# One load per group for batch 0: issued by SyncE, with GpSimd laying out q

## The chip, the cores and the metric

The kernel runs on one NeuronCore of one Trainium2 chip. The metric is the time on the device in microseconds (us), here the median of three runs. One execution was also taken by the hardware profiler; its rows are what the argument rests on. The engines are called by the names of the profile: PE is TensorE (PEld its weight loads), DVE is VectorE, ACT is ScalarE, POOL is GpSimd, SP is SyncE. SPq and ACTq are the instruction streams of SP and ACT where they issue DMAs: an engine that issues a DMA does nothing else in the meantime, and its stream is worked off in order.

## The reference

Two stages in fp32. First attention for 8 batches of 8 heads, 576 tokens, head size 64; heads 0 to 3 see the last 32 tokens, heads 4 to 7 every fourth of the last 128. Then a mixing over the sequence with rank 32 and a two-layer MLP with a residual:

```python
scores = scale * np.matmul(q, k.transpose(0, 1, 3, 2))
scores = np.where(masks[None, :, :, :], scores, -1000000000.0)
...
attn = attn / (np.sum(attn, axis=-1, keepdims=True) + 1e-09)
x = np.matmul(attn, v)          # laid out as [batch, token, head * 64]
h = xt @ U @ V                  # xt is x with tokens last
u = x + h.transpose(0, 2, 1)
return u + np.maximum(u @ w_ch1, 0.0) @ w_ch2
```

U, V, w_ch1 and w_ch2 arrive as 64-bit floats and are read as pairs of 32-bit words, so 16 MB of weights have to be narrowed on the chip.

## The kernel before, in words

**Work.** The 8 x 576 tokens are 36 tiles of 128, and the MLP takes three tiles at a time: 12 chunks, each a loop over 16 blocks f of the hidden layer (`layer1`, L821, and `layer2`, L838), all of it on PE in split precision (three products for each one). Attention of later batches, the mixing and the transposes are put between these matmuls by a queue of due times. So PE has the MLP as its main work from the first L821 to the end.

**Batch 0 comes first.** Nothing of the MLP can start before the first three tiles of x exist, so `first_batch` does batch 0 alone. Its heads are dealt into 9 groups g of 4 units; a unit is two blocks of 64 queries, one in the upper and one in the lower 64 rows of the contraction. For a group, PE multiplies q by k (L394, tile s), DVE masks and takes the row's extreme (L413), ACT takes the exponential (L417, tile p), PE transposes p (L428, tile ptp), ACT copies it to SBUF (L640, tile pt), PE multiplies by v (L451, tile pv), DVE divides (L457 to L481, `place`). The groups are pipelined on PE as s(g), ptp(g-1), pv(g-2). The results of groups 0 to 4 have to be scattered to token order by 24 small DMAs (x<-xp, L485) on SP. After group 7 come the rank-32 products (L517), the mixing (`mix`, L553 and L555) and the transposes of the first three tiles (`transp`, L584, L589, L590), and then the first L821.

**q in batch 0.** The two halves of q must stand in a block-diagonal form, so that the zero blocks keep the two query blocks apart. `q_sb` holds this form for all nine groups: two memsets (L751) clear it once, and two DMAs per group (L305) write the halves. In it the four units lie side by side, so a unit's 128 columns are read with a step of four elements.

**Loads and queues.** `load_q` (one DMA for k, L302, two for q, L305) and `load_v` (L313) are called for all nine groups ahead of everything else, and all of them are issued by ACT. So are all weight pieces: `fetch64` (L179, L181), with 5 raw buffers of which each is 512 KB for a piece. Piece 0 is U, 1 and 2 are V and the rest of U, from 3 on alternating blocks of the two weight matrices. SP issues the masks, the identity, the scatters, and for later batches q, k and v.

**Order.** Within `first_batch`, PE, DVE, ACT and SP keep an order worked out when the program is built; POOL's is by priority. A DMA that is issued waits first for the completion of one some eight DMAs before it, since completions are counted in eight slots shared by both queues (DMAHW0 to DMAHW7 in the rows below). A weight piece goes through ACT twice (L188, L189), DVE twice (L193, L195), and is split into a high and a low part by ACT or DVE (L199, L201) and POOL (L202).

Of the kernel before, what the change touches and what calls it, by code (L numbers as in the profile page):

```python
# [25 lines left out]
P = 128  # L26
# [61 lines left out]
U_AT = (5, 6)  # L88
ORDERED = {mybir.EngineType.PE, mybir.EngineType.DVE, mybir.EngineType.Activation, mybir.EngineType.SP}
# [48 lines left out]
def attention_moe_kernel(ctx: ExitStack, tc: tile.TileContext, q0, k0, qk1, qk2, vv, masks, wide, ident, ut, vt, uv, w1, w2, out):  # L138
# [28 lines left out]
    def fetch64(i):  # L167
        src, n = pieces[i][0], pieces[i][1]
        if 2 * F_LAST <= i - NSMALL:
            raw = [xpool.tile([P, DM], I32, tag="x", name=f"raw{i}_{h}") for h in range(2)]  # L170
        else:
            raw = [prep.tile([P, 2 * DM], I32, tag="raw", name=f"raw{i}", bufs=RAWS)]
        step = 2 * n // len(raw)
        out_ = []
        for h, r in enumerate(raw):
            r = r[:, 0:step]
            if len(src.shape) == 3:
                k = src.shape[1] // len(raw)
                nc.scalar.dma_start(out=r.rearrange("p (a b) -> p a b", a=k), in_=src[:, h * k:(h + 1) * k])  # L179
            else:  # L180
                nc.scalar.dma_start(out=r, in_=src[:, h * step:(h + 1) * step])  # L181
            words = r.rearrange("p (e w) -> p e w", w=2)
            out_.append((words[:, :, 0], words[:, :, 1], slice(h * step // 2, (h + 1) * step // 2)))
        return out_
# [115 lines left out]
    def load_q(g):  # L300
        t = early.tile([P, UNITS, KB], F32, tag="k", name=f"k{g}", bufs=NGB)
        nc.scalar.dma_start(out=t, in_=k0[g])  # L302
        for i in range(2):
            rs = slice(i * QB, (i + 1) * QB)
            nc.scalar.dma_start(out=q_sb[rs, g, i], in_=q0[g, rs])  # L305
        loaded[g, 0] = t

    def load_v(g, i):
        if (g, 1, i) in loaded:
            return  # L310
        if g < NGB:
            t = early.tile([KB, 2, UNITS, VW], F32, tag="v0", name=f"v{g}", bufs=NGB)
            nc.scalar.dma_start(out=t, in_=vv[g])  # L313
            loaded[g, 1, 0] = t[:, 0]
            loaded[g, 1, 1] = t[:, 1]
        else:
            t = work.tile([KB, UNITS, VW], F32, tag="v", name=f"v{g}_{i}", bufs=3)
            ins = nc.sync.dma_start(out=t, in_=vv[g][:, i])
            if g < NGB + 2:
                tc.keep_in_program_order(ins)  # L320
            loaded[g, 1, i] = t
# [47 lines left out]
    def score(g, u):  # L369
# [12 lines left out]
        else:  # L382
# [9 lines left out]
            else:  # L392
                ql, kr = q_sb[:, g].rearrange("p i (q u) -> p u (i q)", u=UNITS)[:, u], loaded[g, 0][:, u]
# [240 lines left out]
    def first_batch():  # L634
# [6 lines left out]

        for g in range(NGB):
            for u in range(UNITS):
                score(g, u)
# [52 lines left out]
        for i in range(0, 2 * TB, 2):  # L697
            fetch(N0 + i, nc.scalar)
# [50 lines left out]
    q_sb = early.tile([P, NGB, 2, UNITS * QB], F32, name="q_sb")  # L749
    for i, eng in enumerate((nc.gpsimd, nc.vector)):  # L750
        eng.memset(q_sb[i * QB:(i + 1) * QB, :, 1 - i], 0.0)  # L751
# [4 lines left out]
    nc.sync.dma_start(out=mask_sb, in_=masks)  # L756
    nc.sync.dma_start(out=id_sb, in_=ident)
    order = tc.manual_schedule(engines=ORDERED)
    order.__enter__()
    for g in range(NGB):  # L760
        load_q(g)
        load_v(g, 0)
# [104 lines left out]
def lay_out(q, k, v, U, V, w1, w2):  # L867
# [6 lines left out]
    for half in range(2):  # L874
# [13 lines left out]
        for i in range(NJ // 2):  # L888
            g = TILES.index((half, 2 * i)) // 2
            for r in (slice(0, D), slice(D, P)):  # L890
                qk2[:, g, :, r, :P] = qp[SPLIT:, :, P * i:P * (i + 1)].transpose(0, 1, 3, 2)
                qk2[:, g, :, r, P:] = kp[SPLIT:, :, P * i:P * i + KW].transpose(0, 1, 3, 2)
    q0 = np.ascontiguousarray(np.stack([q1[0, :, :, i, :, i] for i in range(2)], axis=2)
                              .transpose(0, 2, 3, 4, 1)).reshape(NGB, P, QB * UNITS)
    k0 = np.ascontiguousarray(k1[0].reshape(NGB, UNITS, P, KB).transpose(0, 2, 1, 3))
# [22 lines left out]
    for p in range(NDP):  # L918
# [7 lines left out]
        "q0": q0,  # L926
        "k0": k0,
# [27 lines left out]
```

## Time and profile before

| | us |
|---|---|
| median of 3 runs | 1048.17 (1044.62 to 1048.58) |
| time of the profiled execution | 1047.01 |
| its span, first to last instruction | 1045.1 |
| first score of batch 0 on PE (L394) | 5.95 |
| ACT's first instruction that isn't a DMA | 25.05 |
| last group's scores (g = 8) on PE | 49.91 |
| first matmul of the MLP (L821) | 68.83 |

Times in the profile count from the span's first instruction. The profiled execution took 1.9 us more than its span and is 1.2 us below the median. The granted TensorE clock is 0.986 of full speed over the span. In rows of the timeline the first number is the start, the second the time to the end of the group of merged instructions; brackets give the idle time of the engine before it, and what ended that.

### The profile page before, as it was taken

How to read it: one execution, taken by the hardware profiler on the slowest of the kernel's cores; microseconds unless marked ns; L12 is line 12 of the kernel's file. 1: busy time of each engine (PE TensorE's matmuls, PEld its weight loads, DVE VectorE, ACT ScalarE, POOL GpSimd, SP SyncE). 2: the span in 40 equal slices, each digit the busy share in tenths (PEclk: the TensorE clock that was granted, in tenths of full speed). 3: DMA queues.
4: the chain of work that ended last, by engine and by line, in shares of the span. 5: the costliest groups of instructions: out<-in, count | busy, mean ns of one | idle time of the engine just before them, and what ended most of it. 6: DMA issues, size and time to landing. Idle time of an engine off the chain costs nothing.

```text
span 1045.1 us, 17970 instructions
## 1 busy us (share of the span) xinstructions
PE 990.9 (95%) x5904; PEld 867.7 (83%) x5904; DVE 593.3 (57%) x1972; ACT 387.6 (37%) x946; POOL 298.6 (29%) x501
## 2 busy tenths in 40 slices
PE   1968897899999999999999999999999999999998
PEld 1847785788898888888888888988888888998997
DVE  1359938777536774666637775666737774311211
ACT  0568735434423451434414442434414442111110
POOL 1146613325203350325404351325304340000000
PEclk9989998899999999999999999999999999999999
DMA  9338654434223332434323332433323330400000
GB/s 229 107 119 280 194 161 122 124 101 121 69 67 100 111 98 54 123 95 115 99 67 96 96 109 52 130 97 110 100 70 95 93 91 22 125 1 1 31 1 31
DMA packets 98204, 102.08 MB, mean 98 GB/s; under 512 B 13088, under 2 KB 85984, under 8 KB 98112
## 3 DMA queue, kind: packets, MB, share of 16 engines
q1 hardware_dynamic: 82272, 77.53, 26.6%
q10 hardware_dynamic: 15840, 23.40, 7.3%
q8 instruction: 48, 0.79, 0.3%
q14 instruction: 44, 0.36, 0.1%
HBM read 78.86 MB, written 17.30 MB: 92 GB/s over the span
## 4 chain that ended last, share of the span: by engine, by line
PE 83%; DVE 3%; DMA 2%; issue 1%; ACT 1%; SPq 0%; ACTq 0%; DVEq 0%
PE acc L838 37%; PE ph L821 36%; PE pv L451 4%; PE s L381 3%; PE t L531 2%; PE m L553 1%; DMA raw<-w 1%; PE s L394 1%; DMA zd<-z 1%; DMA v<-vv 0%; DVE v L195 0%; DVE x L555 0%; DVE z L563 0%; PE ptp L428 0%; ACT v L188 0%
## 5 line engine op out<-in xcount | busy, mean ns | idle before, releaser
L838 PE MATMUL acc<-w2h,hh 128*128 128x512 f32 x576 | 229.7, 400 | 8.8 <-ACT hh L826 8.8
L838 PE MATMUL acc<-w2l,hh 128*128 128x512 f32 x576 | 229.3, 399 | 0.0
L827 DVE SCALAR_TENSOR_TENSOR hl<-ph,hh 128x384 fp32r<-128x384 f32 x192 | 106.1, 553 | 199.6 <-ACT hh L826 198.8
L838 PE MATMUL acc<-w2h,hl 128*128 128x512 f32 x576 | 211.3, 399 | 1.1 <-DVE hl L827 1.1
L358 POOL TENSOR_TENSOR qks<-qkr,qks 128x160 fp32r<-128x160 f32 x192 | 102.8, 535 | 367.7 <-ACT qks L357 259.2
L826 ACT ACTIVATE hh<-ph 128x384 fp32r<-128x384 f32 x192 | 93.3, 486 | 268.9 <-PE ph L821 257.4
L821 PE MATMUL ph<-utl,w1h 128*128 128x384 f32 x768 | 175.6, 341 | 0.0
L821 PE MATMUL ph<-uth,w1h 128*128 128x384 f32 x768 | 172.7, 343 | 1.6 <-DVE w1h L201 0.7
L821 PE MATMUL ph<-uth,w1l 128*128 128x384 f32 x768 | 171.8, 340 | 0.5 <-POOL w1l L202 0.5
L417 ACT ACTIVATE p<-p,nmax 128x160 f32<-128x160 f32 (+1 forms) x288 | 109.6, 406 | 132.5 <-DVE nmax L413 131.4
L821 PEld LDWEIGHTS ph<-uth,w1h 128*128 128x128 f32 x768 | 139.4, 191 | 18.7 <-ACT uth L589 1.6
L440 DVE STREAM_TRANSPOSE pt<-p 32x128 f32<-32x128 f32 x432 | 130.1, 301 | 18.7 <-ACT p L417 13.3
L821 PEld LDWEIGHTS ph<-uth,w1l 128*128 128x128 f32 x768 | 137.2, 190 | 1.2 <-POOL w1l L202 0.8
L821 PEld LDWEIGHTS ph<-utl,w1h 128*128 128x128 f32 x768 | 136.0, 189 | 1.7 <-issue 0.2
L838 PEld LDWEIGHTS acc<-w2h,hh 128*128 128x128 f32 x576 | 108.6, 189 | 26.8 <-ACT hh L826 10.6
L838 PEld LDWEIGHTS acc<-w2h,hl 128*128 128x128 f32 x576 | 107.7, 189 | 25.9 <-DVE hl L827 3.3
L838 PEld LDWEIGHTS acc<-w2l,hh 128*128 128x128 f32 x576 | 108.9, 189 | 16.7
L357 ACT CAST qks<-qkr 128x288 fp32r<-128x288 f32 x192 | 81.2, 429 | 95.8 <-PE s L381 53.6
L410 DVE TENSOR_TENSOR p<-s,wide_sb 128x160 f32<-128x160 f32 x192 | 60.1, 320 | 67.9 <-PE s L381 66.1
L361 POOL TENSOR_TENSOR qks<-qkr,qks 64x128 fp32r<-64x128 f32 x192 | 90.6, 472 | 15.0
L500 POOL TENSOR_TENSOR xhl<-x,xhl 128x256 fp32r<-128x256 f32 (+1 forms) x65 | 47.3, 736 | 98.3 <-ACT xhl L498 94.4
L413 DVE CUSTOM_DVE_ANT_0 p<-s,p 128x160 f32<-128x160 f32 x192 | 60.0, 321 | 4.1
(70 smaller groups left out, 868.3 us busy)
## 6 DMA issues: line engine op xcount, KB each, us to landing
qkr<-qk SPq DMA_DIRECT2D x192, 144.0 KB, 2.2
raw<-w ACTq DMA_DIRECT2D x26, 512.0 KB, 5.6
v<-vv SPq DMA_DIRECT2D x126, 97.5 KB, 2.2
out<-x SPq DMA_DIRECT2D x36, 256.0 KB, 2.3
zd<-z SPq DMA_DIRECT2D x120, 64.0 KB, 1.9
xt<-zd SPq DMA_DIRECT2D x30, 256.0 KB, 2.8
qkr<-qk SPq DMA_DIRECT2D x15, 224.0 KB, 4.1
x<-xp SPq DMA_DIRECT2D x96, 32.0 KB, 1.9
```

Of the source, the lines that this page charges most:

```text
L357: nc.scalar.copy(out=t[:, 0:QK2], in_=raw)
L358: nc.gpsimd.tensor_tensor(out=t[:, QK2:], in0=raw[:, P:], in1=t[:, P:QK2].bitcast(F32), op=ALU.subtract)
L361: eng.tensor_tensor(out=t[lo, 0:P], in0=raw[lo, 0:P], in1=t[lo, 0:P].bitcast(F32), op=ALU.subtract)
L410: nc.vector.tensor_tensor(out=p_sb[:, u, :], in0=sp[:, 0:KW], in1=wide_sb[:, kind], op=ALU.add)
L413: nc.vector.tensor_tensor_reduce(out=p_sb[rs, u, 0:w], in0=a, in1=c, scale=-1.0 / 8.0, scalar=3.0e38, op0=ALU.add, op1=ALU.min, accum_out= ...
L417: nc.scalar.activation(out=p_sb[:, u, 0:w], in_=p_sb[:, u, 0:w], func=AF.Exp, bias=nmax[:, u:u + 1], scale=-1.0,)
L440: nc.vector.transpose(out=pt[WIN * k:WIN * (k + 1), :, rs], in_=p_sb[rs, :, o:o + WIN])
L500: eng.tensor_tensor(out=xl[rs], in0=x[rs], in1=xh[rs].bitcast(F32), op=ALU.subtract)
L821: nc.tensor.matmul(ph, lhsT=w[:, k, :], rhs=u[:, k, :], start=(n == 0), stop=(n == len(seq) - 1))
L826: nc.scalar.activation(out=hh, in_=ph, func=AF.Relu)
L827: nc.vector.scalar_tensor_tensor(out=hl, in0=ph, scalar=0.0, in1=hh.bitcast(F32), op0=ALU.max, op1=ALU.subtract)
L838: nc.tensor.matmul(acc[i], lhsT=h[:, ss], rhs=w, start=(f == 0 and n == 0), stop=(f == FC - 1 and n == 2))
```

## The change

Host side: q's two halves and k of a group are laid into one array, `qk0`, as [group, row, unit, 64 of q + 96 of k]. On the chip `load_q` issues one DMA for it on SP instead of three on ACT. The DMA for v is issued by SP too, and so is every weight piece of the whole kernel (`fetch64`) and the first three loads of batch 1. The masks and the identity stay on SP, and now follow group 0's q and k in its stream.

`q_sb` becomes four buffers in rotation, cleared once, each [unit, half, 64], so that a unit's 128 columns lie next to each other. `spread_q` on POOL copies the two halves of a group from the loaded tile into its places; it is called one group ahead of the scores.

```diff
+NQ = 4
...
-                nc.scalar.dma_start(out=r.rearrange("p (a b) -> p a b", a=k), in_=src[:, h * k:(h + 1) * k])
+                nc.sync.dma_start(out=r.rearrange("p (a b) -> p a b", a=k), in_=src[:, h * k:(h + 1) * k])
             else:
-                nc.scalar.dma_start(out=r, in_=src[:, h * step:(h + 1) * step])
+                nc.sync.dma_start(out=r, in_=src[:, h * step:(h + 1) * step])
...
     def load_q(g):
-        t = early.tile([P, UNITS, KB], F32, tag="k", name=f"k{g}", bufs=NGB)
-        nc.scalar.dma_start(out=t, in_=k0[g])
+        t = early.tile([P, UNITS, QB + KB], F32, tag="k", name=f"k{g}", bufs=NGB)
+        nc.sync.dma_start(out=t, in_=qk0[g])
+        loaded[g, 0] = t
+
+    def spread_q(g):
         for i in range(2):
             rs = slice(i * QB, (i + 1) * QB)
-            nc.scalar.dma_start(out=q_sb[rs, g, i], in_=q0[g, rs])
-        loaded[g, 0] = t
+            nc.gpsimd.tensor_copy(out=q_sb[rs, g % NQ, :, i], in_=loaded[g, 0][rs, :, 0:QB])
...
-            nc.scalar.dma_start(out=t, in_=vv[g])
+            nc.sync.dma_start(out=t, in_=vv[g])
...
-                ql, kr = q_sb[:, g].rearrange("p i (q u) -> p u (i q)", u=UNITS)[:, u], loaded[g, 0][:, u]
+                ql, kr = q_sb[:, g % NQ, u].rearrange("p i q -> p (i q)"), loaded[g, 0][:, u, QB:]
...
+        spread_q(0)
         for g in range(NGB):
+            if g + 1 < NGB:
+                spread_q(g + 1)
             for u in range(UNITS):
                 score(g, u)
...
-            fetch(N0 + i, nc.scalar)
+            fetch(N0 + i)
...
-    q_sb = early.tile([P, NGB, 2, UNITS * QB], F32, name="q_sb")
+    q_sb = early.tile([P, NQ, UNITS, 2, QB], F32, name="q_sb")
     for i, eng in enumerate((nc.gpsimd, nc.vector)):
-        eng.memset(q_sb[i * QB:(i + 1) * QB, :, 1 - i], 0.0)
+        eng.memset(q_sb[i * QB:(i + 1) * QB, :, :, 1 - i], 0.0)
...
-    nc.sync.dma_start(out=mask_sb, in_=masks)
-    nc.sync.dma_start(out=id_sb, in_=ident)
...
         load_q(g)
+        if g == 0:
+            nc.sync.dma_start(out=mask_sb, in_=masks)
+            nc.sync.dma_start(out=id_sb, in_=ident)
         load_v(g, 0)
```

The line numbers of the changed kernel are 1 to 7 higher (L302 becomes L303, L394 becomes L397, L821 becomes L828). Three places show what moves in the engines' streams. Numbers behind a name tell buffers apart; k0 is the tile of group 0, p0 its exponentials, raw7 is weight piece 7.

The start of ACT's stream. Before, these rows stand behind 40 rows that issue DMAs, the last of which is shown first:

```order
L179 DMA raw5_164<-w1 128x4x256
L417 ACT_TABLE_LOAD
L417 ACTIVATE p0_166<-p0_166,nmax0_167 128x96 x4
L417 ACTIVATE p1_181<-p1_181,nmax1_182 128x96 x4
L640 COPY pt0_73<-ptp0_188 96x512
```

With the change they are the first rows after the branch into the program:

```order
L957 UNCONDITIONAL_BRANCH
L420 ACT_TABLE_LOAD
L420 ACTIVATE p0_152<-p0_152,nmax0_153 128x96 x4
L420 ACTIVATE p1_169<-p1_169,nmax1_170 128x96 x4
L643 COPY pt0_73<-ptp0_176 96x512
```

All DMA rows of the start have left ACT; what ACT computes keeps its order.

Weight pieces 7 and 8 before the first L821. Before, ACT's stream has their issues behind the three casts of the transposed tiles (uth, L589) and the first weight's high part:

```order
L589 CAST uth0_564<-tp1_576 128x4x128
L589 CAST uth0_564<-tp2_586 128x4x128
L199 CAST w2h_0_80<-v_4_543 128x512
L179 DMA raw7_595<-w1 128x4x256
L338 DMA qkr36_597<-qk1 128x448
L338 DMA qkr38_599<-qk1 128x448
L338 DMA qkr40_601<-qk1 128x448
L218 CAST us_71<-u32_88 128x4x32
L218 CAST us_71<-u32_88 128x32
L188 ACTIVATE v_2_607<-raw2_448 128x448
L189 ACTIVATE raw2_448<-raw2_448 128x448
L188 ACTIVATE v_5_631<-raw5_164 128x512
```

With the change SP's stream has them behind the last scatters, with the waits that stand before each:

```order
L488 DMA x3_265<-xp4_440 32x256 [waits DMAHW7_49]
L488 DMA x4_309<-xp4_440 16x256 [waits DMAHW0_49]
L182 DMA raw2_448<-uv 128x896 [waits DMAHW1_49,Pool_49]
L182 DMA raw6_450<-w2 128x1024 [waits DMAHW2_49,Pool_49]
L180 DMA raw7_595<-w1 128x4x256 [waits DMAHW3_49,Pool_49]
L341 DMA qkr36_597<-qk1 128x448 [waits DMAHW4_49]
L341 DMA qkr38_599<-qk1 128x448 [waits DMAHW5_49]
L341 DMA qkr40_601<-qk1 128x448 [waits DMAHW6_49]
L182 DMA raw8_639<-w2 128x1024 [waits DMAHW7_49,Pool_49]
L180 DMA raw9_728<-w1 128x4x256 [waits DMAHW0_49,DVE_49,Activation_49]
L182 DMA raw10_737<-w2 128x1024 [waits DMAHW1_49,Pool_49]
```

The pieces no longer wait for ACT's turn but for SP's: what SP has to wait for, the rows behind it wait for too, the loads of batch 1 (qkr) among them.

ACT's stream at the same place with the change:

```order
L190 ACTIVATE raw6_450<-raw6_450 128x512
L592 CAST uth0_564<-tp0_566 128x4x128
L190 ACTIVATE raw7_595<-raw7_595 128x512
L592 CAST uth0_564<-tp1_576 128x4x128
L190 ACTIVATE raw8_639<-raw8_639 128x512
L592 CAST uth0_564<-tp2_586 128x4x128
L200 CAST w2h_0_80<-v_4_543 128x512
```

The low words of pieces 6, 7 and 8 are now scaled ahead of and between the three casts that the first L821 waits for; before, pieces 7 and 8 came after it.

More of the change, by code (lines that the diff above doesn't have):

```diff
@@ L137, in attention_moe_kernel @@
 @with_exitstack
-def attention_moe_kernel(ctx: ExitStack, tc: tile.TileContext, q0, k0, qk1, qk2, vv, masks, wide, ident, ut, vt, uv, w1, w2, out):
+def attention_moe_kernel(ctx: ExitStack, tc: tile.TileContext, qk0, qk1, qk2, vv, masks, wide, ident, ut, vt, uv, w1, w2, out):
     nc = tc.nc
@@ L892, in lay_out @@
                 qk2[:, g, :, r, P:] = kp[SPLIT:, :, P * i:P * i + KW].transpose(0, 1, 3, 2)
-    q0 = np.ascontiguousarray(np.stack([q1[0, :, :, i, :, i] for i in range(2)], axis=2)
-                              .transpose(0, 2, 3, 4, 1)).reshape(NGB, P, QB * UNITS)
-    k0 = np.ascontiguousarray(k1[0].reshape(NGB, UNITS, P, KB).transpose(0, 2, 1, 3))
+    q0 = np.stack([q1[0, :, :, i, :, i] for i in range(2)], axis=2).reshape(NGB, UNITS, P, QB)
+    qk0 = np.concatenate([q0, k1[0].reshape(NGB, UNITS, P, KB)], axis=-1)
+    qk0 = np.ascontiguousarray(qk0.transpose(0, 2, 1, 3))
     qk1 = np.concatenate([q1.reshape(B, NGB, UNITS, P, P), k1.reshape(B, NGB, UNITS, P, KB)], axis=-1)
@@ L925, in lay_out @@
     return {
-        "q0": q0,
-        "k0": k0,
+        "qk0": qk0,
         "qk1": qk1,
```

## The prediction

> **What bounds the kernel now.** I read the page's slices first. The third row is ACT, the last the busy share of the 16 DMA engines; a slice is 26 us.
>
> ```profile
> span 1045.1 us, 17970 instructions
> ...
> PE   1968897899999999999999999999999999999998
> ...
> ACT  0568735434423451434414442434414442111110
> ...
> DMA  9338654434223332434323332433323330400000
> ```
>
> PE is full from the ninth slice on; in the first it does a tenth, and ACT nothing, while the DMA engines are at 9. The same by stages (columns: stretch, its length, then busy us of PE, PEld, DVE, ACT, POOL, the granted clock, DMA share, GB/s):
>
> ```profile
> 15.00:20.00 5.00, 0.00 (x0) 0.00 (x0) 0.00 (x0) 0.00 (x0) 0.00 (x0) 1.00 1.07 262
> 20.00:26.00 6.00, 0.00 (x0) 0.00 (x0) 0.00 (x0) 0.94 (x1) 0.00 (x0) 1.00 1.04 251
> ...
> 50.00:69.00 19.00, 12.63 (x95) 8.30 (x96) 9.30 (x34) 8.44 (x19) 4.45 (x4) 0.84 0.15 53
> 69.00:130.00 61.00, 51.24 (x297) 43.92 (x298) 56.88 (x119) 47.66 (x100) 39.53 (x31) 0.94 0.78 251
> 130.00:200.00 70.00, 59.15 (x360) 48.25 (x359) 45.34 (x142) 32.89 (x89) 21.28 (x30) 0.90 0.48 139
> 200.00:1045.00 845.00, 840.29 (x4961) 743.48 (x4959) 468.90 (x1596) 282.09 (x695) 227.31 (x426) 1.00 0.29 81
> ```
>
> From 200 us PE is busy for 840 of 845 us: what starts earlier there ends earlier, by the same amount. From 69 to 130 us DVE is the fullest (56.9 of 61); it narrows the weights. From 15 to 26 us no engine computes. The timeline and the list of waits say why.
>
> ```profile
> 5.95 2.16 PE L394 MATMUL s<-k,q_sb 128*128 128x96 f32 x8 [5.95 <-DMA q_sb<-q]
> ...
> 24.58 0.44 ACTq L179 DMA_DIRECT2D raw<-w  x1
> 25.05 1.28 ACT L417 ACT_TABLE_LOAD   x1 [25.05 <-DMA q_sb<-q]
> 26.35 2.23 ACT L417 ACTIVATE p<-p,nmax 128x96 f32<-128x96 f32 x8
> 26.78 1.24 PE L428 MATMUL ptp<-id_sb,p 128*96 128x128 f32 x4 [16.23 <-ACT p L417]
> 27.81 2.02 PE L394 MATMUL s<-k,q_sb 128*128 128x96 f32 x8
> 31.68 2.19 PE L394 MATMUL s<-k,q_sb 128*128 128x96 f32 x8
> 34.30 1.17 ACT L417 ACTIVATE p<-p,nmax 128x96 f32<-128x96 f32 x4 [1.83 <-DVE nmax L413]
> 38.80 2.11 PE L394 MATMUL s<-k,q_sb 128*128 128x96 f32 x8
> 41.89 2.11 PE L394 MATMUL s<-k,q_sb 128*128 128x96 f32 x8
> ...
> 49.91 2.11 PE L394 MATMUL s<-k,q_sb 128*128 128x96 f32 x8
> ...
> 68.83 1.65 PE L821 MATMUL ph<-uth,w1h 128*128 128x384 f32 x4 [0.68 <-ACT uth L589]
> ```
>
> Scores of groups 0 and 1 are there by 10.5 us, but ACT has all loads and three weight pieces to issue before it may compute, and each issue waits for an earlier DMA's completion. Its first exponential is at 26.35, PE's first transpose waits 16.2 us for it, and everything behind follows from there to the MLP's first matmul at 68.83. The bound of the first 26 us is ACT's stream, not the data of group 0.
>
> **Term 1: batch 0 starts without ACT's issues.** I walk the new start from the rows.
>
> ```profile
> v<-vv ACTq DMA_DIRECT2D x9, 195.0 KB, 4.4
> k<-k ACTq DMA_DIRECT2D x9, 192.0 KB, 4.7
> q_sb<-q ACTq DMA_DIRECT2D x18, 64.0 KB, 4.4
> ...
> mask<-masks SPq DMA_DIRECT2D x1, 240.0 KB, 3.3
> ```
>
> (Size of each DMA, and median us from issue to landing.) Group 0's q and k, 320 KB, are issued first, at about 0.7 us. An early 240 KB took 3.3 us, the later 192 KB took 4.7 in full traffic: I take 3.6, so 4.3 us. POOL then copies two halves of 64 x 256. No row has such a copy; POOL's nearest are these.
>
> ```profile
> 0.74 2.01 POOL L751 MEMSET q_sb<- 64x2304 f32 x1 [0.29 <-POOLq L946]
> ...
> 43.89 0.87 POOL L195 TENSOR_TENSOR u<-u,raw 128x320 int32<-128x320 int32 x1 [39.47 <-ACT raw L189]
> ...
> L361 POOL TENSOR_TENSOR qks<-qkr,qks 64x128 fp32r<-64x128 f32 x192 | 90.6, 472 | 15.0
> ```
>
> The memset goes at 0.87 ns a column, 0.22 us for 256; two-input operations take 2.7 to 3.7 ns a column, 0.7 to 0.9 us for 256. A copy reads one input: I take 0.5, bounds 0.22 and 0.9. Two are 1.0 us (0.45 to 1.8), so the scores of group 0 start at 5.3 instead of 5.95, those of group 1 when the first 2.2 us are over, 7.5. Group 0's exponentials: 2.6 us from a group's scores to the exponential's start (31.68 to 34.30), 1.2 for themselves, so 9.1, before the scores of group 1 end at 9.7. Then a transpose (1.1), and the scores of group 2 start at 10.8 instead of 27.81: 17.0 us earlier.
>
> Is the data there? Up to group 2's q and k stand 1654 KB with masks and identity; at 250 GB/s (the window from 20 us) that is 6.8 us, plus 2 for issue and landing, 8.8, and 9.8 after the copies: in time by 1 us. Up to group 8's they are 5448 KB with U and part of V: 22 us, 24 with landing, against about 30 when they are needed. The cover grows from group to group, so the transfers don't bound it. With a dearer copy (0.9) group 2 would be late by nothing, group 1 by 1 us. POOL's 18 copies are 9 us on an engine that idles from 4.5 to 43.9 us; they bind only if two take longer than a group's period.
>
> From group 2 to group 8 it was 22.1 us. PE's clock state stays as it was for the first ten us of work (3.87 us a group, against 3.09 from 38.80 on). What changes is the weight load of the scores, as q's columns now lie side by side:
>
> ```profile
> L394 PEld LDWEIGHTS s<-qkr x120: 186/192/192, 84.1 to 823.5; 128*128 128x128 f32 x120
> ...
> L394 PEld LDWEIGHTS s<-k,q_sb x72: 307/329/332, 5.9 to 51.5; 128*128 128x128 f32 x72
> ...
> 84.12 1.51 PE L394 MATMUL s<-qkr 128*128 128x96 f32 x12
> ```
>
> (ns, smallest/median/largest.) Twelve score matmuls with q side by side took 1.5 us in batch 1, so eight take 1.0 instead of 2.1. That is at most 1.1 us for each of four groups, 4.4. But ACT has 1.2 of exponentials, 0.6 of copy and in two groups 1.0 of narrowing, 1.8 to 2.8 a group, and comes to be the bound of a period near 2. I take 1.8 us, bounds 0 and 4.4. Group 8's scores end 18.8 us earlier.
>
> **What could hold it back up to the first L821.** The scatters on SP:
>
> ```profile
> 35.57 16.90 SPq L485 DMA_DIRECT2D x<-xp  x24
> ...
> 57.70 0.42 DVE L555 TENSOR_TENSOR x<-x,m 128x256 f32<-128x256 f32 x1 [1.39 <-PE m L553]
> ```
>
> 24 took 16.9 us, 0.7 each. They would start near 19 us, 3.9 behind the scores of group 3 as before (31.68, 35.57). But they now stand in one queue behind the loads and three weight pieces, and with eight slots the eighth of them waits until the last piece has landed. Loads and pieces together are 7179 KB, 29 us at 250 GB/s; the new loads have larger packets, so I take 28. Another 16 issues of 0.7 end at 39, landed by 41. The addition that needs them moves from 57.70 to 39: here a new wait of about 2 us comes up. Pieces 6, 7 and 8 follow the scatters on SP, and their first use now stands in ACT's stream before the casts that L821 waits for.
>
> ```profile
> 68.26 0.39 ACTq L179 DMA_DIRECT2D raw<-w  x1
> ...
> 70.43 0.33 ACTq L181 DMA_DIRECT2D raw<-w  x1
> ...
> 31.81 0.66 ACT L189 ACTIVATE raw<-raw 128x512 int32<-128x512 uint32 x1
> ...
> raw<-w ACTq DMA_DIRECT2D x26, 512.0 KB, 5.6
> ```
>
> Two more such activations are 1.3 us on that path, and piece 8, issued at about 46 after three loads of batch 1, lands at 51 to 52, when the last cast is due at 49.4 + 2. I charge 4 us for all this (2 for the scatters, 1.3, and the rest for piece 8), bounds 0 and 9 (a whole landing of 5.6 more than the scatters' 2 and the 1.3). Term 1: 18.8 - 4 = 15 us; first L821 at 54.
>
> **Term 2: weights in chunk 0.** Pieces 7 and 8 were issued at 68.26 and 70.43; now at about 44 and 46, that is 24 us earlier while the MLP starts 15 earlier. The MLP's second block would find its weights waiting, and DVE, which is the fullest engine of this stage, gets its work sooner. ACT also loses the issue of pieces 9 to 28, 0.35 us each, 7 us of a stage in which it is busy for 47.7 of 61: idle time of an engine that isn't the bound. I take 3 us, bounds 0 and 9, the difference of the two shifts.
>
> **Sum:** 1047.0 of the profiled execution - 15 - 3 = **1029 us**. The median of before is 1.2 higher, within the spread of its runs.
>
> The Trainium skill, "DMA: Bandwidth & Descriptors", section "Issuing engines are not separate DMA queues", says that DMAs of all issuers run on the same 16 engines, and that issuing from several saves only issue time, usually small beside the transfer. By that, moving them would gain almost nothing, 1046. The row of ACT's table load at 25.05 bears against it here, because issuing also holds up the engine's own work.
>
> **Rivals.**
>
> 1. *SP's stream holds batch 1 back, slower.* In chunk 0 the weight pieces now stand in one stream with q, k and v of batch 1, and wait for free raw buffers there.
>
> ```profile
> SPq L338 <- DMA raw<-w: 35.1, 4, 25.5
> ...
> qkr<-qk SPq DMA_DIRECT2D x15, 224.0 KB, 4.1
> ```
>
> If a load comes behind two pieces (5.6 us to landing against its own 4.1, and a buffer's wait), PE, which works in order, stands at the scores. Each of nine groups would have to lose more than 18 / 9 = 2 us to turn the sign. At 3 us a group the time is 1047 - 18 + 27 = 1056. Against it: in the order shown the loads stand close to where they stood in time, and SP had idle time there (35.1 us in the row).
>
> 2. *The one queue eats half of it ahead of L821.* Scatters and piece 8 come late to their bound, 9 us, q's layout is worth nothing, and term 2 nothing: 1047 - 17 + 9 = 1039. Here belongs a first copy that is late: the Trainium skill, "GPSIMD Engine Reference", section 2.1 "Instruction dispatch", tells of about 6 us for the first call into freshly loaded code. POOL's row at 43.89 stands behind 39 us of idle time and can't show such a wait; if it fell on group 0, the time by it would be about 1035.
>
> 3. *More than forecast.* All 9 us of term 2, the wait of 2 us for the scatters doesn't come up, and 2.6 more from q's layout: 1029 - 6 - 2 - 2.6 = 1018.
>
> 4. *No effect:* the loads, not their issue, set the pace, and batch 0 ends when it did. It would take group 8's data 20 us longer than now; 1047. The windows at 250 GB/s speak against it.
>
> **Chances.** Forecast 0.60; rival 3 0.14; rival 2 0.17; rival 1 0.06; rival 4 0.03. The range 1018 to 1040 holds all but the last two and the edges. About 0.5% (5 us) is what a measurement of this kernel tells from no change: faster 0.91, same 0.03, slower 0.06.
>
> **What would show it.** ACT's table load in the first 2 us; the scores of group 2 near 11, of group 8 near 30; weight loads of s near 190 ns at full clock; first L821 near 54; the stage to the end of chunk 0 not longer than before. It is wrong if PE waits at L397 for DMAs in chunk 0, if L821 comes after 60, or if PE isn't full from about 180 us on.

## The result, and the profile after

The changed kernel takes 1029.23 us (median of 4 runs, 1027.74 to 1031.81), the kernel before 1046.86 (4 runs, 1044.62 to 1048.58): ratio 0.9835, with a 95% interval of 0.9806 to 0.9865. The forecast was 1029. The profiled execution took 1031.81 us with a span of 1029.3, so it is the slowest of the four; another one had a span of 1025.8.

In the page's slices (25.7 us each; PE, ACT, DMA) the first slice of PE now shows 7 where it showed 1:

```profile
span 1029.3 us, 17998 instructions
...
PE   7589986999999999999999999999999999999998
...
ACT  5477445344233441434323541434323442111110
...
DMA  9558445343223422333233422334223421400000
```

The timeline of the start, with the rows that stood in the prediction for the kernel before (start, us, engine, line; L397 was L394, L420 was L417, L828 was L821):

```profile
0.74 1.28 ACT L420 ACT_TABLE_LOAD   x1 [0.74 <-PEq L952]
3.98 0.84 POOL L309 COPY q_sb<-k 64x256 f32<-64x256 f32 x2 [0.64 <-DMA k<-qk]
4.88 2.02 PE L397 MATMUL s<-k,q_sb 128*128 128x96 f32 x8 [4.88 <-POOL q_sb L309]
7.24 1.17 ACT L420 ACTIVATE p<-p,nmax 128x96 f32<-128x96 f32 x4 [5.21 <-DVE nmax L416]
7.74 0.85 POOL L309 COPY q_sb<-k 64x256 f32<-64x256 f32 x2 [2.92 <-DMA k<-qk]
11.32 1.86 PE L397 MATMUL s<-k,q_sb 128*128 128x96 f32 x8
14.87 1.13 PE L397 MATMUL s<-k,q_sb 128*128 128x96 f32 x8
...
25.38 0.86 POOL L309 COPY q_sb<-k 64x256 f32<-64x256 f32 x2 [2.06 <-DMA k<-qk]
26.34 0.87 POOL L196 TENSOR_TENSOR u<-u,raw 128x320 int32<-128x320 int32 x1
27.26 1.91 PE L520 MATMUL t<-xp,u 128*32 128x256 f32 x8 [1.54 <-POOL u L196]
29.10 1.13 PE L397 MATMUL s<-k,q_sb 128*128 128x96 f32 x8
...
53.17 1.65 PE L828 MATMUL ph<-uth,w1h 128*128 128x384 f32 x4 [0.68 <-ACT uth L592]
```

ACT's table load has gone from 25.05 to 0.74, the first exponential from 26.35 to 7.24, the scores of group 2 from 27.81 to 11.32, those of group 8 from 49.91 to 29.10, the first matmul of the MLP from 68.83 to 53.17. The stages (columns as in the prediction):

```profile
15.00:20.00 5.00, 5.00 (x64) 4.50 (x65) 2.95 (x22) 3.35 (x11) 1.58 (x4) 1.00 1.04 284
...
50.00:69.00 19.00, 13.96 (x49) 11.59 (x50) 15.29 (x22) 13.08 (x28) 13.23 (x12) 0.68 0.48 162
69.00:130.00 61.00, 58.88 (x379) 51.29 (x377) 50.51 (x131) 40.47 (x90) 30.84 (x24) 0.97 0.67 212
130.00:200.00 70.00, 57.31 (x337) 46.88 (x337) 49.89 (x152) 33.80 (x88) 24.56 (x38) 0.85 0.44 126
200.00:1029.00 829.00, 824.84 (x4859) 730.22 (x4857) 458.05 (x1555) 275.66 (x679) 221.38 (x414) 1.00 0.29 80
```

PE is now at work all of 15 to 20 us, where no engine computed. At the other end nothing changed: PE is busy for 824.8 of the last 829 us. The whole difference lies ahead of that. The timelines of all the kernels that were run give these points (us; "scatters" are those of batch 0 on SP, first start and end of the row; chunk 0 reaches from the first matmul of the MLP to that of chunk 1; "clock" is the granted TensorE clock over chunk 0, of full speed):

| kernel | table load | s of group 8 | scatters | first MLP matmul | chunk 0 | clock | span |
|---|---|---|---|---|---|---|---|
| before | 25.05 | 49.91 | 35.57, 52.47 | 68.83 | 126.7 | 0.93 | 1045.1 |
| before, second profile | 25.53 | 51.30 | 36.05, 53.81 | 70.27 | 126.1 | 0.93 | 1045.7 |
| after | 0.74 | 29.10 | 21.09, 41.27 | 53.17 | 126.5 | 0.89 | 1029.3 |
| after, second profile | 0.74 | 28.55 | 20.65, 41.10 | 53.17 | 123.9 | 0.93 | 1025.6 |
| issuer alone | 0.74 | 32.03 | 26.08, 44.13 | 56.54 | 129.0 | 0.90 | 1034.9 |
| merged and contiguous, on ACT | 17.26 | 36.34 | 26.57, 43.72 | 59.37 | 127.2 | 0.89 | 1035.8 |
| three transfers, contiguous, on SP | 0.74 | 30.86 | 28.73, 46.68 | 58.97 | 124.2 | 0.91 | 1032.2 |
| later pieces on ACT | 0.74 | 26.38 | 18.89, 39.93 | 52.25 | 130.6 | 0.89 | 1032.1 |
| first pieces on ACT too | 0.74 | 33.85 | 18.43, 38.76 | 51.02 | 130.0 | 0.91 | 1029.0 |
| scatters half on ACT | 0.74 | 40.76 | 21.18, 40.53 | 58.33 | 128.1 | 0.89 | 1036.1 |
| scatters half on POOL | 0.75 | 30.94 | 21.15, 33.46 | 55.21 | 126.6 | 0.90 | 1030.4 |
| additions left out | 0.74 | 27.61 | 20.82, 40.28 | 52.30 | 113.7 | 0.95 | 1014.6 |
| additions partly on POOL | 0.74 | 27.81 | 20.64, 40.64 | 52.84 | 127.5 | 0.89 | 1029.7 |
| neither hold | 0.75 | 29.95 | 20.42, 33.86 | 47.38 | 127.0 | 0.90 | 1023.5 |

From chunk 1's first matmul to the end of the span it is 848 to 850 us in each. Two kernels therefore differ by two lengths: the time up to the first MLP matmul, and chunk 0. The first was measured to 1.5 us by two profiles of the same kernel (68.83 and 70.27; 53.17 twice), the second to 2.6 us (126.5 and 123.9). In these last two the granted clock differs as well, 0.89 and 0.93; PE is busy for 108.7 and 105.8 us of chunk 0.

### The profile page after: what moved, and what is told of

The parts are those of the page before. It is cut to its first block, busy times and chain, and to the rows that moved or that the text cites. A ratio compares the mean times of both kernels' runs of the same rounds, so it can differ in the third digit from the quotient of the medians.

```text
span 1029.3 us, 17998 instructions
## 1 busy us (share of the span) xinstructions
PE 988.1 (96%) x5904; PEld 864.9 (84%) x5904; DVE 593.6 (58%) x1972; ACT 387.4 (38%) x946; POOL 306.7 (30%) x519
## 4 chain that ended last, share of the span: by engine, by line
PE 85%; DVE 2%; DMA 1%; ACT 1%; issue 0%; POOL 0%; DVEq 0%; SPq 0%; ACTq 0%
PE acc L845 38%; PE ph L828 37%; PE pv L454 4%; PE s L384 3%; PE t L534 2%; PE m L556 1%; PE s L397 1%; DMA raw<-w 1%; DVE v L196 1%; DMA zd<-z 0%; DVE v L194 0%; DVE x L870 0%; ACT v L189 0%; DVE z L566 0%; DVE x L558 0%
## 5 line engine op out<-in xcount | busy, mean ns | idle before, releaser
L834 DVE SCALAR_TENSOR_TENSOR hl<-ph,hh 128x384 fp32r<-128x384 f32 x192 | 106.2, 553 | 189.9 <-ACT hh L833 189.2
L828 PE MATMUL ph<-utl,w1h 128*128 128x384 f32 x768 | 176.6, 343 | 0.0
L828 PE MATMUL ph<-uth,w1h 128*128 128x384 f32 x768 | 172.7, 343 | 3.2 <-DVE w1h L202 1.6
L828 PE MATMUL ph<-uth,w1l 128*128 128x384 f32 x768 | 173.6, 342 | 0.7 <-POOL w1l L203 0.7
L420 ACT ACTIVATE p<-p,nmax 128x160 f32<-128x160 f32 (+1 forms) x288 | 109.8, 406 | 133.8 <-DVE nmax L416 132.4
L828 PEld LDWEIGHTS ph<-uth,w1h 128*128 128x128 f32 x768 | 139.5, 191 | 20.4 <-DVE w1h L202 1.8
L828 PEld LDWEIGHTS ph<-uth,w1l 128*128 128x128 f32 x768 | 138.0, 191 | 1.8 <-POOL w1l L203 1.0
L828 PEld LDWEIGHTS ph<-utl,w1h 128*128 128x128 f32 x768 | 137.5, 191 | 1.7 <-issue 0.2
```

Of the source, the lines that this page charges most:

```text
L420: nc.scalar.activation(out=p_sb[:, u, 0:w], in_=p_sb[:, u, 0:w], func=AF.Exp, bias=nmax[:, u:u + 1], scale=-1.0,)
L828: nc.tensor.matmul(ph, lhsT=w[:, k, :], rhs=u[:, k, :], start=(n == 0), stop=(n == len(seq) - 1))
L834: nc.vector.scalar_tensor_tensor(out=hl, in0=ph, scalar=0.0, in1=hh.bitcast(F32), op0=ALU.max, op1=ALU.subtract)
```

## Experiments: the two halves of the change

*Theory:* the gain is ACT's stream being free of issues. *Rival:* it is the transfers, their number and layout, and the issuer does not matter. The first kernel takes the issuer alone from the change:

```diff
-        nc.scalar.dma_start(out=t, in_=k0[g])
+        nc.sync.dma_start(out=t, in_=k0[g])
...
-            nc.scalar.dma_start(out=q_sb[rs, g, i], in_=q0[g, rs])
+            nc.sync.dma_start(out=q_sb[rs, g, i], in_=q0[g, rs])
```

and so for v, the pieces and batch 1's first loads; the masks and the identity follow group 0's loads as in the change.

> The first half of the change alone: everything that ACT issued before is issued by SyncE, but q keeps its own two transfers per group and its place with a step of four elements; GpSimd copies nothing. Theory 1 (freeing ACT's stream is what gains, the layout gives the 4 us between group 2's and group 8's scores): ACT's table load within 2 us, group 2's scores at about 12 us, group 8's at 33 to 34 instead of 29.1, first L821 of the MLP at 56 to 57, time 1032 to 1035. Theory 2 (fewer and larger transfers are what gains): batch 0 waits for its loads, first MLP matmul at 63 or later, 1041 to 1044.

Measured: 1035.79 us against 1051.31 of before on that chip, ratio 0.9872 (0.9836 to 0.9907). Theory 2 is out: the first MLP matmul came at 56.54, not at 63 or later. Group 2's scores came at 11.83 and group 8's at 32.03, 2.9 us behind the change's where theory 1 said 4, and the time is 0.8 us above its range. The second takes the merged load and POOL's copies alone, and ACT issues as before:

```diff
-        nc.sync.dma_start(out=t, in_=qk0[g])
+        nc.scalar.dma_start(out=t, in_=qk0[g])
```

> The second half alone: one transfer for q and k of a group and GpSimd's copies as in the change, but every load and weight piece is issued by ACT as before. Theory 1: ACT still has 23 issues ahead of its first exponential instead of 40; it comes at about 21 us instead of 26.4, group 8's scores at about 40, first MLP matmul at 59 to 60, time 1037 to 1040. Theory 2: most of the gain is here, 1030 to 1034.

Measured: 1036.42, ratio 0.9876 (0.9817 to 0.9936). ACT has 23 issues ahead of its first computation in place of 41 (the trace of the kernel before has 41, not 40), and its table load comes at 17.26:

```profile
16.84 0.39 ACTq L180 DMA_DIRECT2D raw<-w  x1
17.26 1.28 ACT L420 ACT_TABLE_LOAD   x1 [17.26 <-DMA raw<-vt]
```

The table load and group 8's scores (36.34) came some 4 us earlier than theory 1 said, the first MLP matmul (59.37) where it said; the 1030 to 1034 of theory 2 were not reached. So each half alone gives some three quarters of the ratio's gain (1.3 and 1.2 of 1.65%), and they overlap: both shorten the time until ACT may compute, one by taking the issues away, one by having fewer of them.

What does the merging add once SP issues? The third kernel keeps the change, but loads k and each half of q by a transfer of its own, contiguous, and has no POOL copies:

```diff
-        nc.sync.dma_start(out=t, in_=qk0[g])
+        nc.sync.dma_start(out=t, in_=qk0[g][:, :, QB:])
+        for i in range(2):
+            rs = slice(i * QB, (i + 1) * QB)
+            nc.sync.dma_start(out=q_sb[rs, g, :, i], in_=qk0[g, rs, :, 0:QB])
```

> The changed kernel with three transfers for each group's q and k, in place of one and two copies on GpSimd: k, and each half of q straight into its place beside the zeros (q's columns contiguous for TensorE as in the changed kernel, 64 float32 a packet); nine buffers in place of four, all issued by SyncE. If the merging matters (41 issues in place of 23 on SyncE, which after 8 of them waits for completions): the scatters start 4 to 5 us later than 21.1, as in the kernel where only the issuer was changed (26.1), the first matmul of the MLP comes at 55.5 to 57 in place of 53.2, and the time is 1032 to 1036. If q's layout was what that kernel lacked: its scores take 1.1 us for eight, group 8's scores come at 28 to 30, and the time is 1028 to 1031.

Measured: 1034.97, ratio 0.9862 (0.9838 to 0.9886). SP has to issue 1.83 us for each group's q and k:

```profile
24.59 0.55 SPq L303 DMA_DIRECT2D k<-qk  x1
25.18 1.28 SPq L306 DMA_DIRECT2D q_sb<-qk  x2
...
28.73 17.95 SPq L489 DMA_DIRECT2D x<-xp  x24
...
DVE x L559 <- DMA x<-xp: 7.3, 1, 7.3
```

(The last row is from the list of waits, us in total, times, longest.) Its scores are as early as the change's to within 2 us (30.86), but the scatters stand behind the 41 issues, start at 28.73 in place of 21.09 (7.6 us later, where 4 to 5 were expected), and DVE waits 7.3 us for them. Contiguous q makes a group 1.0 us shorter where the loads keep up (groups 3 to 5 follow every 2.1 us, and every 3.1 in the kernel with the issuer alone); groups 6 and 7 then wait 0.9 and 1.8 us for their q, so that 1.2 us are left at group 8's scores (32.03 to 30.86). The merging is worth 5.8 us at the first MLP matmul (58.97 to 53.17), more than the 2.3 to 3.8 expected. The bytes are the same; the delay stands in SP's row of issues. The forecast knew the issues as ACT's problem; on SP, too, they are a stream that something waits behind.

## Experiments: what holds the first MLP matmul back

Between group 8's scores and the first MLP matmul lie 18.9 us before and 24.1 after. These rows of the changed kernel's timeline show what is new there: DVE waits twice for scatters, and ACT three times for pieces 6, 7 and 8, whose low words it scales ahead of the three casts of uth.

```profile
38.19 0.42 DVE L558 TENSOR_TENSOR x<-x,m 128x256 f32<-128x256 f32 x1 [1.73 <-DMA x<-xp]
41.31 0.42 DVE L558 TENSOR_TENSOR x<-x,m 128x256 f32<-128x256 f32 x1 [1.29 <-DMA x<-xp]
...
46.30 0.65 ACT L190 ACTIVATE raw<-raw 128x512 int32<-128x512 uint32 x1 [3.74 <-DMA raw<-w]
...
48.31 0.68 ACT L190 ACTIVATE raw<-raw 128x512 int32<-128x512 uint32 x1 [0.88 <-DMA raw<-w]
...
51.35 0.67 ACT L190 ACTIVATE raw<-raw 128x512 int32<-128x512 uint32 x1 [1.08 <-DMA raw<-w]
```

That is 3.0 us on DVE and 5.7 on ACT. Two kernels change who issues the pieces, and when. In the first ACT issues piece 2 and those from 6 on:

```diff
+        eng = nc.scalar if i == 2 or i >= NSMALL + 3 else nc.sync
...
-                nc.sync.dma_start(out=r, in_=src[:, h * step:(h + 1) * step])
+                eng.dma_start(out=r, in_=src[:, h * step:(h + 1) * step])
```

> The change, but the second part of U and V and all weight pieces from 6 on are issued by ACT, in its stream where they stood before. Tells what the one queue costs ahead of the MLP, and what early pieces 7 and 8 are worth in chunk 0. Theory 1 (the early pieces are worth nothing and ACT's wait for them costs 2 to 3 us): first MLP matmul at 50 to 51 instead of 53.2, chunk 0 as long as before (126.5 us to the first matmul of chunk 1), time 1026 to 1028. Theory 3 (chunk 0 ends as its weights come): chunk 0 is longer by what L821 is earlier, 1029 to 1031.

Measured: 1031.34, ratio 0.9837 (0.98 to 0.9873). In the second ACT also issues the first three weight pieces, at group 4:

```diff
+        eng = nc.scalar if i >= 2 else nc.sync
...
+            if g == 4:
+                send(NSMALL + 3)
```

> As the kernel before it in this set, and the first three weight pieces are issued by ACT too, at group 4 of batch 0, so that SyncE's stream has only q, k, v and U ahead of the scatters. Theory 1: the scatters start at about 18.5 us instead of 21 and end by 36 instead of 41, DVE's wait of 3 us for them is gone, first MLP matmul at 48 to 49, time 1024 to 1027. Theory 3: chunk 0 gives it back, 1028 to 1031.

Measured: 1031.32, ratio 0.9834 (0.98 to 0.9869). The first MLP matmul comes 0.9 and 2.2 us earlier than in the change, both later than theory 1 said, and chunk 0 is longer by 3.5 us and more, as theory 3 said, so that the time can't be told from the change's. In the first, the casts of uth stand free of pieces, but ACT waits 3.1 us for piece 6 (sent at 30.13) further ahead, before its activation at 35.48. In the second, three issues on ACT, with the waits between them, take it from 20.31 to 25.04, and group 5's exponentials wait behind them; group 8's scores move to 33.85:

```profile
20.31 0.44 ACTq L181 DMA_DIRECT2D raw<-w  x1
...
24.61 0.39 ACTq L181 DMA_DIRECT2D raw<-w  x1
25.04 1.17 ACT L421 ACTIVATE p<-p,nmax 128x96 f32<-128x96 f32 x4 [4.24 <-DMA k<-qk]
```

By then the first MLP matmul had come 12 us behind the last scatter in four kernels (after 11.9, issuer alone 12.4, these two 12.3), which made SP's row of scatters look like the bound. Two kernels tested that; every second scatter of batch 0 goes to another engine, ACT in the one and POOL (`nc.gpsimd`) in the other:

```diff
-        for t, to, n, r in sorted(moves):
-            nc.sync.dma_start(
+        for k, (t, to, n, r) in enumerate(sorted(moves)):
+            eng = nc.scalar if b == 0 and k % 2 else nc.sync
+            eng.dma_start(
```

> The changed kernel, with every second one of batch 0's 24 scatters of the dilated half issued by ScalarE in place of SyncE. If SyncE's row of scatters (21.1 to 41.3 us) sets the first matmul of the MLP, which came 12 us behind the last scatter in four kernels: the last scatter goes out at about 36 to 38, the first matmul at 49 to 50 in place of 53.2, 3 to 4 us earlier. If something else sets it (ScalarE's row of exponentials and casts): the scatters end earlier and the first matmul stays at 53 or comes later, since 12 issues of 0.4 to 0.7 us are now in ScalarE's stream, 5 to 8 us. Time: 1025 to 1029 by the first, 1029 to 1036 by the second.

> The changed kernel with every second one of batch 0's 24 scatters issued by GpSimd in place of SyncE (on ScalarE they held the exponentials, as the loads did before). If the row of scatters sets the first matmul of the MLP: the last one goes out at 31 to 36 in place of 41.3, and the first matmul comes at 45 to 50, 3 to 8 us earlier than 53.2; the time is 1022 to 1027, as long as chunk 0 doesn't give it back. If the narrowing and the casts in ScalarE's row set it, the first matmul stays at 52 to 54 and the time at 1028 to 1031. If GpSimd's issues take 1.5 us or more each or hold its copies of q: later than 54.

Measured: on ACT 1037.54, ratio 0.9893 (0.9848 to 0.9938); on POOL 1033.01, ratio 0.9843 (0.9819 to 0.9867); the change on the same chip as the first 1029.42, ratio 0.9821 (0.978 to 0.9861). On ACT the issues stand in front of the exponentials, and group 8's scores go to 40.76: the kernel before in small.

```profile
22.35 2.84 ACTq L489 DMA_DIRECT2D x<-xp  x2
25.24 1.17 ACT L420 ACTIVATE p<-p,nmax 128x96 f32<-128x96 f32 x4 [7.62 <-DMA k<-qk]
...
26.81 4.11 ACTq L489 DMA_DIRECT2D x<-xp  x3
```

On POOL the scatters end 7.8 us earlier (13 on SP take 12.3 us), no DVE addition waits for them, and yet the first MLP matmul comes 2 us later, at 55.21. **The theory of the scatters falls**, and 55.21 lies in none of the three forecasts (GpSimd's issues took 0.5 us each, so they are not the reason for coming later than 54). In this kernel the order that is worked out at build time has the low word of piece 6 ahead of a cast of ts in ACT's stream, and ACT waits there for the piece; what made the order differ is not shown. Group 8's last pv and all behind it follow 4 us later, at half the clock (granted 0.50 from 38 us on, against 0.99 to 42 us in the change):

```profile
33.56 0.53 SPq L182 DMA_DIRECT2D raw<-uv  x1
34.18 0.38 SPq L182 DMA_DIRECT2D raw<-w  x1
...
38.44 0.65 ACT L190 ACTIVATE raw<-raw 128x512 int32<-128x512 uint32 x1 [4.07 <-DMA raw<-w]
...
40.13 1.14 PE L454 MATMUL pv<-v,pt 96*64 96x65 f32 x16 [4.18 <-ACT pt L644]
```

The wait for piece 6 stood there in the first kernel with pieces on ACT too. The new theory: two waits hold, the scatters in DVE's stream and the pieces in ACT's, and taking one away leaves the other. The last kernel takes both: half of the scatters on POOL, and the pieces from 6 on issued by ACT, the early sending of piece 6 dropped, so that no low word of theirs stands ahead of a cast.

```diff
+        eng = nc.scalar if i >= NSMALL + 3 else nc.sync
...
-        for t, to, n, r in sorted(moves):
+        for k, (t, to, n, r) in enumerate(sorted(moves)):
+            eng = nc.gpsimd if b == 0 and k % 2 else nc.sync
...
-                send(NSMALL + 4)
```

> The changed kernel with both waits between group 8's scores and the first matmul of the MLP taken out. Every second scatter of batch 0 goes over GpSimd, as in the run before, which ended the scatters at 33.5 in place of 41.3 and yet gave 55.2; and the weight pieces from the fourth on are issued by ScalarE behind the three casts of uth (the early sending of the fourth is dropped), so that no narrowing of them stands ahead of a cast. In the profile of the changed kernel VectorE waits 3.0 us for scatters there and ScalarE 5.7 us for pieces. If these two waits are the hold-back: 53.2 - 3.0 - 5.7 = 44.5, with TensorE at half its clock there 45 to 48. If only one of them counts, or the work itself at half the clock sets it: 50 or later. The weights then come later to chunk 0, and VectorE and GpSimd, which bound it, are late by as much: chunk 0 gives part of it back (126 to 132), and the time is 1021 to 1029; if it gives back all, as in the two kernels with pieces on ScalarE, 1029 to 1032.

Measured: 1024.90 us (5 runs, 1023.71 to 1026.72), ratio 0.9788 (0.977 to 0.9806).

```profile
41.27 0.58 ACT L594 CAST uth<-tp 128x512 fp32r<-128x512 f32 x1 [1.65 <-PE tp L589]
...
46.74 0.58 ACT L594 CAST uth<-tp 128x512 fp32r<-128x512 f32 x1 [2.26 <-PE tp L589]
...
47.38 1.65 PE L829 MATMUL ph<-uth,w1h 128*128 128x384 f32 x4 [0.68 <-ACT uth L594]
```

The three casts (at 41.27, 43.90 and 46.74) stand one behind the other with nothing of the pieces between, and the first MLP matmul comes at 47.38: 17.4 us behind group 8's scores in place of 24.1, 5.8 earlier than in the change and within the 45 to 48 expected. PE did not run at half its clock all the way (granted 0.88 between these two points, against 0.77 in the change), but that is a small part of it: the three groups of transposes ahead of the casts take 0.66, 0.89 and 1.11 us here and 1.11, 1.11 and 1.12 in the change, and in the change's second profile, at 0.66, the stretch is only 0.6 us longer (24.6). What the runs don't show is each wait's own share: no kernel takes the pieces' wait away and leaves the scatters as they were. Chunk 0 is 127.0, next to 126.5 and 123.9 in the change, so most of the gain stays. It is the fastest complete kernel of the study, about 4.4 us under the change by the medians; the two were not run on one chip, and their ratios to before lie side by side (upper end 0.9806, lower ends 0.9806 and 0.978), so the size of that step is less sure than its place in the trace.

## Experiments: what bounds chunk 0

Term 2 expected chunk 0 to become shorter by 3 us because its weights come earlier, and in the profiled pair it did so by 0.2. *Theory:* VectorE's work bounds it, not the arrival. One kernel leaves the low-word additions of w1 and w2 out:

```diff
-            add_low(i - 2, nc.vector)
+            narrow_b([], pipe[i - 2][1], nc.vector)
+            added.add(i - 2)
```

> The changed kernel without VectorE's additions of the weights' low words (the line `eng.tensor_tensor(... op=ALU.add)` for the pieces of w1 and w2; their shift stays). It leaves out the low words of the weights. In the changed kernel these additions stand between the shift and the casts, on the engine that is busy for 29 of 31 us at the head of chunk 0. If VectorE's work bounds chunk 0 (126.5 us from the first matmul of the MLP to the first of chunk 1, of which TensorE computes about 103): chunk 0 becomes shorter by 8 us or more, to 118 or less, and the run takes 1021 or less. If the arrival of the pieces bounds it (term 2 of the prediction): chunk 0 stays within 3 us of 126.5, and the run at 1026 to 1030. The start, up to the first matmul of the MLP, stays at 53.

Measured: 1018.17, ratio 0.9708 (0.9669 to 0.9747); chunk 0 113.7 us. Two windows of 31 us behind the start of chunk 0, first of the second profile of the change, then of this kernel:

```profile
53.00:84.00 31.00, 27.23 (x128) 24.30 (x129) 29.17 (x55) 24.47 (x52) 23.16 (x19) 0.88 0.70 231
84.00:115.00 31.00, 28.32 (x189) 23.88 (x187) 29.48 (x69) 23.27 (x50) 19.75 (x13) 1.00 0.71 221
```

```profile
53.00:84.00 31.00, 30.52 (x170) 27.39 (x170) 25.43 (x50) 29.84 (x63) 25.22 (x22) 0.95 0.93 307
84.00:115.00 31.00, 31.00 (x223) 26.90 (x222) 18.26 (x66) 18.65 (x44) 12.79 (x11) 1.00 0.56 172
```

With the additions DVE is at 29 of 31 and PE at 27 to 28; without them DVE falls to 25 and 18, and PE is full. Chunk 0 gets shorter by 10 to 13 us, as the theory said. Pieces 6 to 8 are sent as early as in the change, 11 to 9 us ahead of the first MLP matmul; the later ones follow sooner, the last by 7 us, since a piece waits for one of the five raw buffers and these come free as it is narrowed. So the narrowing on DVE bounds chunk 0, and with it the sending of most pieces. To gain from this with nothing left out, the next kernel gives every third of these additions to POOL:

```diff
-            add_low(i - 2, nc.vector)
+            add_low(i - 2, nc.gpsimd if i % 3 == 0 and i < NSMALL + 18 else nc.vector)
```

> The changed kernel with the low-word addition of every third of the first 18 weight pieces on GpSimd in place of VectorE. Leaving all of these additions out made chunk 0 shorter by 10 to 13 us (113.7). Six of them, 0.96 us each, are 5.8 us less on VectorE in chunk 0, and 6 times about 1.7 us, 10 us more on GpSimd, which is busy for 43 of the 62 us after the first matmul. If VectorE alone bounds the stage: chunk 0 at 118 to 121 in place of 124 to 126, the time 1023 to 1025. If the longer way of a piece over GpSimd binds instead (its subtraction of 1.5 us stands there too): chunk 0 at 124 or longer, 1029 to 1034.

Measured: 1032.21, ratio 0.9831 (0.9803 to 0.9858), chunk 0 127.5. It gains nothing, as the second forecast had it, and DVE's rows say why: four of the six additions fell into chunk 0, and from 53 to 145 us DVE's 20 remaining ones take 1163 ns each, against 1084 and 964 for 24 in the first and the second profile of the change.

```profile
L196 DVE CUSTOM_DVE_ANT_0 v<-raw,v 128x1024 uint16<-128x1024 uint16 x20 | 23.2, 1163 | 0.4
```

Four additions fewer, and 23.2 us of DVE where the two profiles of the change have 25.9 and 23.0. What stretches them is in the section on the hardware.

Two more runs show how far profiles of one kernel differ: the change and the kernel before once more.

> The changed kernel itself once more, beside the others on one chip: 1029 by all theories, first matmul of the MLP at 53, chunk 0 at 126.5 us. If chunk 0 differs by more than 1 us between two profiles of this kernel, differences of that size between the kernels are no evidence.

> The kernel before itself, profiled once more. Two profiles of the changed kernel gave 126.5 and 123.9 us for chunk 0, with the same first matmul of the MLP (53.17 both). By all theories: first matmul of the MLP at 68 to 70, the chain of the start as before (first exponential at 26). Term 2 compares chunk 0 of the two kernels: if this profile gives 126 to 127 again, the earlier weight pieces are worth 0 to 2.7 us; if it differs by 2 us or more from 126.7, the two kernels can't be told apart in that stage by single profiles.

Measured: the change 1029.42 (1028.09 to 1032.56), ratio 0.9821 (0.978 to 0.9861), chunk 0 123.9 where the first profile had 126.5; before 1047.36, ratio to itself 0.9982 (0.9959 to 1.0006), chunk 0 126.1 where it had 126.7. A difference of chunk 0 of up to 2.6 us between single profiles is therefore no evidence by itself.

## Why the prediction was right, and where it was not

- **What bounds the start: right.** The issuer alone brings the table load to 0.74 and 1.3% of the time, and wherever issues were put back on ACT (merged loads, the first pieces, half of the scatters) the exponentials behind them were late again by what the issues took. The sentence of the Trainium skill that was weighed ("DMA: Bandwidth & Descriptors", "Issuing engines are not separate DMA queues"), by which the time would be 1046, does not agree with the 1029.2 measured: it counts the issue time against the transfers, and here the cost was what stands behind the issues in the issuer's own stream.
- **Term 1, 15 us: right in sum** (15.7 at the first MLP matmul, 17.1 by the second profiles), from parts that err against each other: group 8's scores came 20.8 us earlier (18.8 forecast), and the hold-back behind them took 5.2 (4). That the total meets the forecast to 0.2 us is luck in this sense.
  - Group 2's scores came at 11.32 (10.8 forecast), the copies took 0.42 each (0.5), the first as soon as its load was there, so the wait for a first call on POOL that the second rival names did not show.
  - Group 8's came at 29.10 (about 30): 17.8 us behind group 2's in place of 22.1, so 4.3 us were gained there and not 1.8, nearly the upper bound of 4.4. The period near 2 came (2.1 us from group 3 to group 7), but ACT was not its bound: from 15 to 20 us PE is busy for all 5.0 us and ACT for 3.35. The slow first ten us of PE's work came too: its eight score matmuls take 2.02 us at 4.88, 1.86 at 11.32 and 1.13 from 14.87 on. But they now fall on groups 0 to 2, while before, behind the wait of 16.2 us, groups 2 and 3 were slow again (3.9 and 4.0 us in place of 3.1), and the prediction left that stretch in its 22.1. "The transfers don't bound it" failed too: POOL waits 2.9 us for group 1's load and 2.1 for group 8's, and as it works in order, the addition for U waits behind those copies, PE's t matmuls wait 1.5 us for U, and group 8's scores stand behind them. A copy whose data is late holds all that POOL has behind it; the prediction costed the copies but not what queues behind them.
  - q's layout was taken at 1.8 us (0 to 4.4), of at most 1.1 a group; between the two kernels with three transfers on SP it measured 1.0 a group, and 1.2 in all at group 8's scores, where waits for loads took the rest.
  - The hold-back was taken at 4 us (0 to 9) and measured 5.2. Its makers were named rightly, scatters behind the loads (2 forecast, 3.0 us of waits on DVE), narrowings of pieces 6 to 8 ahead of the casts and their landing (2 forecast, 5.7 us of waits on ACT, which partly lie beside DVE's). That taking away one of them is not enough, and that both together give 5.8 us, is what the runs add.
  - What the prediction didn't price is the merging for SP: 41 issues there would have cost 5.8 us at the first MLP matmul.
- **Term 2, 3 us: its size is not shown, and its mechanism was half right.** "The MLP's second block would find its weights waiting" came true: its first matmul comes 4.3 us behind that of the first block in both profiles of the change (57.44 in the first), where it came 7.7 (76.51) and 7.9 behind in those of the kernel before. But only pieces 7 and 8 come sooner to the MLP. Piece 9 waits for a raw buffer and is sent 3.6 us behind the first MLP matmul (56.80), before 4.2 (73.00). "DVE gets its work sooner" finds little room: in the first two stretches of 31 us of chunk 0 DVE is busy for 28.8 and 30.1 us, before for 27.5 and 30.3. What is left at the end of chunk 0 depends on the pair of profiles: 0.2 us with the change at the lower clock (0.89 against 0.93), 2.2 to 2.8 with both at 0.93. The medians differ by 17.6 us, of which the first MLP matmul has 15.7 to 17.1. So between nothing and the 3 us is possible, and no run settles it.
- **The rivals.** SP's stream held nothing back in chunk 0: in the whole run PE's weight loads waited for a DMA at L397 once, 0.4 us, at 29.10 and so ahead of it. The second rival's hold-back of 9 us, the third's term 2 of 9 us, and no effect did not come.

What stays open: why chunk 0 is 130 us in the two kernels with pieces on ACT and 127.0 in the last one, which has them there too, at nearly the same clock (0.89, 0.91 and 0.90). The orders of the engines differ between all of these kernels.

## What to carry to other kernels

A DMA issue is an instruction of the engine that issues it: count the issues that stand ahead of an engine's first useful instruction, on the idle engine too, because something waits behind them there as well. When one wait is removed, list the others that end at nearly the same time; here taking one alone away brought 2 us at best and cost 2 in another kernel. And where a stage is bound by an engine's work, don't count on earlier data for the whole stage: here the first blocks started sooner, and at the end 0 to 3 us were left. Leave the work out once, to see what it is worth, before moving it.

## What the runs showed of the hardware

VectorE's shifts and additions did not run beside GpSimd's work in chunk 0. The second profile of the change, both engines at 62 to 67 us (start, us):

```profile
61.86 1.52 DVE L194 TENSOR_SCALAR v<-v 128x512 int32<-128x512 int32 x1
63.41 1.64 DVE L196 CUSTOM_DVE_ANT_0 v<-raw,v 128x1024 uint16<-128x1024 uint16 x1
64.97 0.41 DVE L194 TENSOR_SCALAR v<-v 128x512 int32<-128x512 int32 x1
65.42 0.69 DVE L196 CUSTOM_DVE_ANT_0 v<-raw,v 128x1024 uint16<-128x1024 uint16 x1
...
61.73 1.36 POOL L203 TENSOR_TENSOR w2l<-v,w2h 128x512 fp32r<-128x512 f32 x1
63.05 1.45 POOL L203 TENSOR_TENSOR w1l<-v,w1h 128x512 fp32r<-128x512 f32 x1
65.78 1.47 POOL L203 TENSOR_TENSOR w2l<-v,w2h 128x512 fp32r<-128x512 f32 x1 [1.28 <-ACT w2h L200]
```

The same shift takes 1.52 us where POOL is at work when it starts and 0.41 where POOL is idle; the same addition 1.64 and 0.69. The longer ones end 0.3 and 0.55 us after the POOL instruction that was under way at their start, which is near what they take by themselves: they wait for it. Not all of DVE's work does: from 53 to 145 us of this profile the shift takes 1.27 us in the median with POOL at work at its start (15 times) and 0.42 without (11), but `hl` (L834), which reads PSUM, takes 0.55 in both cases. DVE's 29 busy us of 31 are in part such waits. The Trainium skill, "SBUF — State Buffer", section "Who interferes with whom", describes it: VectorE and GpSimd share a pair of SBUF ports; an instruction that takes the pair holds it for its whole length, and the other engine is blocked meanwhile. These rows agree, and so does the kernel that moved additions to POOL and made DVE's own ones longer (1163 ns). The prediction took DVE and POOL as two engines with their own idle time.

Issues cost more on SP than they looked to: in the kernel with two more small ones for each group, the loads of the groups took 0.55 to 0.65 us each to issue from the second group on, where the change's mostly took 0.33 to 0.43. On POOL a scatter took 0.51 us to issue (median of 11), against 0.59 on SP (of 181).

An issue does not stop what its engine has already begun. In the kernel before, ACT's issue of piece 7 (68.26, 0.39 us) lies inside its cast of uth (68.19, 0.58 us); the cast behind the issue starts at 68.68, when the issue has ended. So it is what stands behind an issue in the stream that has to wait.
